# Chunked attention and a routed expert layer on one core: q and k of a tile in one transfer, V of two tiles in one

## The chip, the cores and the metric

The kernel runs on one core of a Trainium2 chip. The metric is the device time of one execution in microseconds (us). Engines are named as in the profile: PE is TensorE (matmul), PEld its weight load, DVE is VectorE, ACT is ScalarE, POOL is GpSimd, SP is SyncE, whose queue issues nearly all transfers between memory and SBUF. DMA share is the mean busy share of the core's 16 DMA engines.

## The reference

Inputs are q, k and v of 8 batches, 8 heads, 576 positions and 64 dimensions, in float32. Attention is computed in chunks of 64 positions. Its output, 4608 tokens of 512 values, goes through a layer of 8 experts: a token with a positive skip score is sent to its best expert, the others are passed through.

```python
scores = scale * np.matmul(q_c, k_c.transpose(0, 1, 2, 4, 3))   # chunks of 64
attn = np.exp(scores - max); attn = attn / (sum + 1e-09)
x = np.matmul(attn, v_c)                     # then 4608 tokens of 512
do_compute = x @ w_skip > 0
e_idx = np.argmax(x @ w_gate)                # of the tokens that compute
h = np.maximum(x @ w1[e], 0.0)
out = x + gate * (h @ w2[e])                 # of those; the others are x
```

## The kernel before, in words

The tokens are 36 tiles of 128 (NT, 128 rows each, two chunks of 64). The first stage, up to about 130 us, is the attention, in a loop over i from 0 to 38 that is a software pipeline: in iteration i, PE computes the scores of tile i (pe_scores, line 234, matmuls of line 241), transposes the probabilities of tile i-2 (pe_ptrans, line 273), multiplies those of tile i-3 with V (pe_pv, line 281, matmuls of line 289), transposes the output of tile i-4 (pe_xt, line 316), and computes router logits of older tiles (lines 328 and 341). ACT copies and exponentiates between these steps, DVE takes maxima and divides, POOL subtracts maxima. Routing work of groups of tiles is laid between. The second stage runs the experts' matmuls (lines 519 and 551), on tokens that POOL gathers from the output by indirect transfers, with weights loaded by SP in pieces of 512 KB (line 209).

The order of work on each engine is the order in which the program is written (a manual schedule), and a wait is put in by the framework where an instruction needs another's result or a buffer that is still in use. An engine that waits holds up everything behind it in its own order.

The input of a tile comes in three transfers, all issued by SP. load_q (line 124) takes a new buffer "st" out of five (QK_AHEAD) and loads q of the tile, 256 KB, 2048 bytes a partition; load_k (line 128) loads k into the other half of the same buffer; load_v (line 131) loads V with a column of ones, 260 KB, 2080 bytes a partition, into a buffer "sv" out of six (V_AHEAD). Ahead of the loop (lines 139 to 149) SP issues the first five q and k, the constants "csb" and "rsb", and six V. In the loop, q of tile i+5 is issued at the start of iteration i, behind pe_scores of tile i, which frees the buffer (line 735); the row of an output tile, or half a piece of expert weights, by side() (lines 304 to 310, and 360); V of tile i+3 behind pe_pv of tile i-3, which frees that buffer (line 766); and k of tile i+5 at the end (line 767).

SP's transfers take turns on eight semaphores (DMAHW0 to DMAHW7), and a transfer waits until the one eight before it on SP has landed. So at most eight of SP's transfers are in flight. PE starts with ten warm-up matmuls (line 160), with which the first loads run.

Of the kernel before, what the change touches and what calls it, by code (L numbers as in the profile page):

```python
# [9 lines left out]
F32 = mybir.dt.float32  # L10
# [8 lines left out]
P = 128  # L19
B, H, S, D = 8, 8, 576, 64  # L20
CH = 64
NTOK = B * S
NT = NTOK // P
# [3 lines left out]
KC = DM // P  # L27
# [28 lines left out]
QK_AHEAD = 5  # L56
V_AHEAD = 6
# [46 lines left out]
def moe_attention_kernel(ctx: ExitStack, tc: tile.TileContext, qk: bass.AP, vo: bass.AP, cst: bass.AP, crow: bass.AP, wall: bass.AP, out: bass.AP):  # L104
    nc = tc.nc
# [8 lines left out]
    ap = apool.__enter__()  # L114
# [5 lines left out]
    T = [dict() for _ in range(NT)]  # L120
    lgs = {}
    halves = (slice(0, CH), slice(CH, P))

    def load_q(t):
        T[t]["st"] = ap.tile([P, 2, DM], F32, name="st", bufs=QK_AHEAD)
        nc.sync.dma_start(T[t]["st"][:, 0], qk[0, t])

    def load_k(t):
        nc.sync.dma_start(T[t]["st"][:, 1], qk[1, t])

    def load_v(t):
        T[t]["sv"] = ap.tile([P, 2 * KC, D + 1], F32, name="sv", bufs=V_AHEAD)
        nc.sync.dma_start(T[t]["sv"].rearrange("p h d -> p (h d)"), vo[t])

    man = tc.manual_schedule()
    man.__enter__()
    csb = cpool.tile([P, CCOLS], F32, name="csb")
    rsb = cpool.tile([1, RCOLS], F32, name="rsb")
    for t in range(QK_AHEAD):
        load_q(t)  # L140
        load_k(t)
        if t == 1:
            nc.sync.dma_start(csb, cst)
        if t == 2:
            nc.sync.dma_start(rsb, crow)
        if t >= 2:
            load_v(t - 2)
    for t in range(QK_AHEAD - 2, V_AHEAD):
        load_v(t)
# [8 lines left out]
    def pe_warm(n):  # L158
        for _ in range(n):
            nc.tensor.matmul(warm, ones, zeros, start=True, stop=True)  # L160
# [32 lines left out]
    def more_constants():  # L193
        nc.vector.tensor_copy(upper, C("upper"))
        nc.vector.tensor_copy(cbase, C("cbase"))
        nc.vector.tensor_copy(recs[:, 0:2], C("tok").rearrange("p (c t) -> p c t", c=2))
        nc.vector.tensor_copy(dcon, csb[:, _C["wdesc"][0]:_C["iota"][1]])
        nc.vector.memset(ecum[:, 0, :], 0.0)
        nc.vector.memset(onesf, 1.0)
# [28 lines left out]
    def fill(q, budget):  # L228
        while q and budget >= 0.5 * q[0][0]:
            c, _, f = q.pop(0)  # L230
            f()
            budget -= c
# [59 lines left out]
    def ve_x(t):  # L292
        xq = T[t].pop("xq")[:, :, :XW].rearrange("p a (j d) -> p a j d", j=KC)
        rr = spool.tile([P, 2, KC, 1], F32, name="rr", bufs=2)
        nc.vector.tensor_scalar(rr, xq[:, :, :, D:], 1e-9, None, op0=ALU.add)
        nc.vector.reciprocal(rr, rr)
        x = ap.tile([P, DM], F32, name="xa", bufs=X_BUFS)
        nc.vector.tensor_tensor(x.rearrange("p (j a d) -> p a j d", a=2, d=D), xq[:, :, :, :D], rr.to_broadcast([P, 2, KC, D]), op=ALU.mult)  # L298
        rows.append((t, x))
        T[t]["x"] = x  # L300
# [3 lines left out]
    def side(i, n):  # L304
        for _ in range(n):
            if pieces and (pieces[0] < FC and i in W_AT or i >= BURST and pieces[0] >= FC and (not rows or pieces[0] <= (i - BURST) * 2 + FC)):
                load_half(pieces.pop(0))
            elif rows:
                t, x = rows.pop(0)
                nc.sync.dma_start(out[t * P:(t + 1) * P, :], x)  # L310
# [52 lines left out]
    def conv_half():  # L363
        st, hi, lo = cws.pop(0)
        nc.scalar.activation(hi, st, AF.Copy, scale=SW)
        fd.append((600, None, lambda: nc.vector.scalar_tensor_tensor(lo, st, SW, hi, op0=ALU.mult, op1=ALU.subtract)))

    def pool_lo():
        hi, st, lo = pl.pop(0)
        nc.gpsimd.tensor_tensor(lo, st, hi, op=ALU.subtract)  # L370
# [280 lines left out]
    def on(f, t):  # L651
        if 0 <= t < NT:
            f(t)
# [26 lines left out]
    def stage(g):  # L680
        next(jobs[g])
# [27 lines left out]
    def u0_mm():  # L709
        fc, n = u0[0], units[0][3]  # L710
        u0[0] += 1
        hp = u0_bank(fc)[:, :n]
        for m, (a, b, j) in enumerate((a, b, j) for a, b in ((0, 0), (0, 1), (1, 0)) for j in range(KC)):
            nc.tensor.matmul(hp, wsets[0][:, a, fc, j * P:(j + 1) * P], xt0[:, b, j, :n], start=(m == 0), stop=(m == 11))
        u0_ev.append((hp, fc))

    def u0_out():
        l1_out(ht0, *u0_ev.pop(0), units[0][3])

    def early_xt():  # L720
        return [blk_xt(xt0[:, :, :, m * P:(m + 1) * P], xgs[m], xp=u0_bank(m)) for m in range(2)]

    def do(i, spot):
        for f, a in spots.pop((i, spot), ()):
            f(*a)

    def conv_pool():
        st, hi, lo = cws.pop(0)
        nc.scalar.activation(st, st, AF.Copy, scale=SW)
        nc.scalar.activation(hi, st, AF.Copy)  # L730
        pl.append((hi, st, lo))

    for i in range(NT + 3):
        on(pe_scores, i)
        on(load_q, i + QK_AHEAD)
        if i == 2:
            more_constants()
        wm = WARM[i + 1] if i + 1 < len(WARM) else (0, 0, 0, 0)
        pe_warm(wm[0])
        on(ve_max, i - 1)  # L740
        if i != NT + 1:
            on(ve_x, i - 4)
        side(i, 1 if i < BURST else 2)
        if i % 2 == 0:
            on(ve_logit, i - 8)
        do(i, "d")
        if i == NT + 1:
            for f in lows:
                f()
        fill(fd, 600)  # L750
        do(i, "p")
        pe_warm(wm[1])
        on(ac_scores, i)
        on(pe_ptrans, i - 2)
        on(ac_pt, i - 2)
        do(i, "m")
        on(ac_exp, i - 1)
        pe_warm(wm[2])
        while pl:
            pool_lo()  # L760
        for c in range(W_CONV.count(i)):
            conv_half() if i < NT - 2 else conv_pool()
        pe_warm(wm[3])
        on(pe_pv, i - 3)
        if i >= 3:
            on(load_v, i - 3 + V_AHEAD)
        on(load_k, i + QK_AHEAD)
        if i >= BURST:
            side(i, 2)
        if i == NT + 2:  # L770
            ve_x(NT - 1)
            stage(5)
        if i % 2 == 0:
            on(pe_logit, i - 6)
            on(ac_logit, i - 6)
        if i % 2:
            on(pe_ltrans, i - 7)
        on(pe_xt, i - 4)
        on(ac_xt, i - 4)
        do(i, "e")  # L780
        if i == NT:
            ve_x(i - 3)
            scpool.__exit__(None, None, None)
            upool = tc.tile_pool(name="ps_u", bufs=1, space=PSUM, reuse_waits="tile")
            ps_u = upool.__enter__()
            lows = early_xt()
        if i > NT:
            u0_mm()
        if u0_ev and i > NT + 1:
            u0_out()  # L790
# [136 lines left out]
    for i, (p, bs, offs, n) in enumerate(units):  # L927
# [21 lines left out]
        for k, (b, o) in enumerate(zip(bs, offs)):  # L949
# [4 lines left out]
            for _ in l2_steps(y, hc, w, o, nb):  # L954
# [3 lines left out]
                if todo and at >= total - 1 - (TLEAD if i else LLEAD) * len(todo):  # L958
                    m, o2 = todo.pop(0)
# [45 lines left out]
def lay_out(q, k, v, moe_w_skip, moe_w_gate, moe_w1, moe_w2):  # L1005
    nch = S // CH

    def cols(a):
        a = a.reshape(B, KC, 2, nch, CH, D).transpose(0, 3, 5, 1, 2, 4).reshape(NT, 2, D, KC, 2, CH).copy()
        a[:, :, :, :, 1] = a[:, ::-1, :, :, 1]  # L1010
        return a.reshape(NT, P, DM)

    vv = v.reshape(B, KC, 2, nch, CH, D).transpose(0, 3, 2, 4, 1, 5).reshape(NT, 2, P, KC, D).transpose(0, 2, 1, 3, 4)
    vo = np.ones((NT, P, 2, KC, D + 1), np.float32)
    vo[..., :D] = vv
    vo = vo.reshape(NT, P, 2 * KC * (D + 1))
    qk = np.ascontiguousarray(np.stack([cols(q), cols(k)]))
    cst, crow = constants()
    wsg = np.concatenate([moe_w_skip[:, None], moe_w_gate], axis=1)
    lo, hi = _C["wsg"]  # L1020
    wp = np.zeros((P, KC, WP), np.float32)
    wp[:, :, :NE + 1] = wsg.reshape(KC, P, NE + 1).transpose(1, 0, 2)
    cst[:, lo:hi] = wp.reshape(P, -1)
    w1 = moe_w1.reshape(NE, KC, P, FC, P).transpose(0, 3, 2, 1, 4).reshape(NE, FC, P, KC * P)
    w2 = moe_w2.reshape(NE, FC, P, DM)
    wall = np.ascontiguousarray(np.concatenate([w1, w2], axis=3))
    return {"in_qk": qk, "in_vo": vo, "in_cst": cst, "in_crow": crow, "in_wall": wall}
# [14 lines left out]
```

## Time and profile before

| What | us |
|---|---|
| median of three runs | 350.34 (345.41 to 353.88) |
| profiled execution, its own time | 348.78 |
| its span, first to last instruction | 347.0 |
| PE busy in the span | 322.8 (93%) |
| DVE, ACT, POOL busy | 242.4, 195.1, 131.2 |
| q and k: 72 transfers of 256 KB, median from issue to landing | 5.0 |
| V: 36 transfers of 260 KB | 5.1 |
| output rows: 36 of 256 KB | 5.2 |
| weights: 56 of 512 KB | 4.2 |

The profile is of one execution. A row of the timeline gives the start, the length, the engine, the line and operation, the tiles written and read, and in square brackets how long the engine had been idle and what ended that; "issue" means that nothing in the profile explains it. A row of waits gives the engine and line, what it waited for, the total in us, how many times, and the longest. In the windows each engine has its busy time and in brackets its number of instructions; behind them stand the granted PE clock (1.00 is full speed), the DMA share and GB/s. In rows of transfers the last number is the median time from issue to landing in us. "q1 hardware_dynamic" is the queue of SP's transfers, "q8 instruction" one that carries program code.

### The profile page before, as it was taken

To read this page: it belongs to the slowest core of one execution; us is meant where nothing else is said; L and a number is where in the kernel's file an instruction comes from. 1 tells how busy PE (TensorE), PEld (TensorE's weight loads), DVE (VectorE), ACT (ScalarE), POOL (GpSimd) and SP (SyncE) were. 2 spreads that over 40 slices of the span, in tenths; PEclk is the share of its full clock that TensorE was granted. 3 is DMA by queue.
4 is the path that set the end of the run, shared out by engine and by line. 5 is a ranking of instruction groups with operands and counts; after the bars stand their busy time and mean duration, and the time that the engine had idled before them with its cause. 6 is when DMAs were issued, how large, how long until landed. Compare 5 with 4: busy or idle time off the path is not lost. (4 is left out here: it accounts for less than half of the span.)

```text
span 347.0 us, 10921 instructions
## 1 busy us (share of the span) xinstructions
PE 322.8 (93%) x4388; PEld 221.0 (64%) x4388; DVE 242.4 (70%) x539; ACT 195.1 (56%) x345; POOL 131.2 (38%) x158
## 2 busy tenths in 40 slices
PE   7889898998997999999999999999999999999980
PEld 3567676776675777659555446647647658587750
DVE  1645676987796887987889857876777779667420
ACT  3777787987784895516546344545444445455210
POOL 4423354463637456845050532242343353020111
PEclk9999999999998999999999999999999999999996
DMA  7999999998997992039375877668658767574000
GB/s 237 394 388 362 378 324 321 329 359 291 311 318 256 301 368 95 2 107 383 109 266 170 288 250 238 189 191 270 193 179 278 226 205 228 183 230 133 33 26 29
DMA packets 34408, 81.86 MB, mean 236 GB/s; under 512 B 4255, under 2 KB 4256, under 8 KB 34354
## 3 DMA queue, kind: packets, MB, share of 16 engines
q1 hardware_dynamic: 31250, 71.79, 62.1%
q0 software_dynamic: 3104, 9.33, 7.6%
q8 instruction: 36, 0.59, 0.7%
q14 instruction: 18, 0.15, 0.2%
HBM read 67.07 MB, written 14.17 MB: 234 GB/s over the span
## 5 line engine op out<-in xcount | busy, mean ns | idle before, releaser
L551 PE MATMUL sp<-wset,ht 128*128 128x512 f16 (+7 forms) x552 | 102.8, 379 | 0.0
L519 PE MATMUL hp<-xt,wset 128*128 128x288 f16 (+6 forms) x768 | 85.9, 273 | 0.9 <-DVE ht L528 0.9
L519 PEld LDWEIGHTS <-wset 128*128 128x128 f16 x768 | 69.3, 98 | 18.3 <-issue 3.4
L551 PEld LDWEIGHTS <-ht 128*128 128x128 f16 (+7 forms) x552 | 45.6, 101 | 45.1 <-issue 2.1
L218 DVE SCALAR_TENSOR_TENSOR wset<-wst,wset 128x1024 f16<-128x1024 f32 x56 | 67.6, 1217 | 9.2 <-ACT wset L217 9.1
L221 POOL DMA_INDIRECT out<-x,recsi x18 | 24.3, 1351 | 101.1 <-DVE x L561 87.7
L217 ACT ACTIVATE wset<-wst 128x1024 f16<-128x1024 f32 x56 | 57.8, 1048 | 1.8 <-DMA wst<-in_wall 1.8
L253 POOL TENSOR_TENSOR px<-sc,mx 128x512 f32<-128x512 f32 x36 | 38.0, 1058 | 53.4 <-DVE mx L251 30.6
L527 ACT ACTIVATE ht<-hp 128x288 f16<-128x288 f32 (+6 forms) x64 | 24.5, 383 | 56.0 <-PE hp L519 54.8
L528 DVE SCALAR_TENSOR_TENSOR ht<-hp,ht 128x288 f16<-128x288 f32 (+6 forms) x64 | 26.1, 422 | 17.9 <-ACT ht L527 17.3
L251 DVE TENSOR_REDUCE mx<-sc 128x8 f32<-128x512 f32 x36 | 24.4, 678 | 19.7 <-ACT sc L246 19.1
L503 ACT ACTIVATE xt<-xt 128x512 f16<-128x512 f32 (+7 forms) x20 | 10.3, 513 | 43.3 <-PE xt L502 43.3
L289 PE MATMUL xq<-sv,pz 64*64 64x65 f32 x1152 | 27.4, 226 | 6.5 <-issue 5.8
L289 PEld LDWEIGHTS xq<-sv,pz 64*64 64x64 f32 x1152 | 21.6, 135 | 13.6 <-issue 10.6
L241 PE MATMUL sc<-st 64*64 64x64 f32 x1152 | 25.9, 227 | 3.2 <-DMA st<-in_qk 1.8
L322 ACT ACTIVATE xc<-sp 128x512 f32<-128x512 f32 x36 | 21.4, 595 | 11.4 <-PE sp L316 10.1
L241 PEld LDWEIGHTS sc<-st 64*64 64x64 f32 x1152 | 20.9, 136 | 10.7 <-issue 4.6
L246 ACT ACTIVATE sc<-sc 128x512 f32<-128x512 f32 x36 | 21.5, 597 | 9.9 <-PE sc L241 8.6
L298 DVE TENSOR_TENSOR xa<-xq,rr 128x512 f32<-128x512 f32 x36 | 24.9, 692 | 1.2
L221 POOL DMA_INDIRECT xg<-out,recsi x18 | 23.2, 1287 | 5.5 <-issue 3.7
L273 PE MATMUL sp<-csb,px 128*128 128x128 f32 x144 | 23.9, 289 | 0.4 <-ACT sc L246 0.4
L506 DVE SCALAR_TENSOR_TENSOR xt<-xt 128x512 f16<-128x512 f32 (+7 forms) x20 | 11.7, 585 | 17.2 <-ACT xt L503 16.7
(157 smaller groups left out, 374.0 us busy)
## 6 DMA issues: line engine op xcount, KB each, us to landing
wst<-in_wall SPq DMA_DIRECT2D x56, 512.0 KB, 4.2
st<-in_qk SPq DMA_DIRECT2D x72, 256.0 KB, 5.0
sv<-in_vo SPq DMA_DIRECT2D x36, 260.0 KB, 5.1
out<-xa SPq DMA_DIRECT2D x36, 256.0 KB, 5.2
wst<-in_wall SPq DMA_DIRECT2D x16, 256.0 KB, 5.2
csb<-in_cst SPq DMA_DIRECT2D x1, 312.5 KB, 5.0
xg<-out,recsi POOLq DMA_INDIRECT x18, 5.6
out<-x,recsi POOLq DMA_INDIRECT x18, 4.8
```

What stands on the lines that cost most here:

```text
L217: nc.scalar.activation(w[:, 0, fc, :], st, AF.Copy, scale=SW)
L218: nc.vector.scalar_tensor_tensor(w[:, 1, fc, :], st, SW, w[:, 0, fc, :], op0=ALU.mult, op1=ALU.subtract)
L221: ins = nc.gpsimd.indirect_dma_start(**kw)
L241: nc.tensor.matmul(sp[halves[c], a, j], st[halves[r], 0, w], st[halves[r], 1, w], start=(j == 0), stop=True, skip_group_check=True)
L251: nc.vector.tensor_reduce(mx, T[t]["sc"], axis=AX.X, op=ALU.max)
L253: nc.gpsimd.tensor_tensor(px, T[t].pop("sc"), mx.unsqueeze(2).to_broadcast([P, H, CH]), op=ALU.subtract)
L289: nc.tensor.matmul(xq[w, a, j * (D + 1):(j + 1) * (D + 1)], pz[r, j, w], v[r, c, j], start=(j == 0), stop=True, skip_group_check=True)
L298: nc.vector.tensor_tensor(x.rearrange("p (j a d) -> p a j d", a=2, d=D), xq[:, :, :, :D], rr.to_broadcast([P, 2, KC, D]), op=ALU.mult)
L519: nc.tensor.matmul(hp, w()[:, a, fc, j * P:(j + 1) * P], xt[:, b, j, :n], start=(m == 0), stop=(m == 11))
L527: nc.scalar.activation(ht[:, 0, fc, :n], hp, AF.Relu)
L528: nc.vector.scalar_tensor_tensor(ht[:, 1, fc, :n], hp, 0.0, ht[:, 0, fc, :n], op0=ALU.max, op1=ALU.subtract)
L551: nc.tensor.matmul(y[c * P // cg:c * P // cg + n], ht[:, a, fc, o:o + n], w[:, b, fc, P * KC:], start=(f == 0 and m == 0), stop=(f == fw - ...
```

## The change

q and k of a tile lie side by side in memory and are loaded by one transfer of 512 KB, 4096 bytes a partition, into the same buffer "st" as before. V of two tiles lies side by side and is loaded by one transfer of 520 KB, 4160 bytes a partition (532 thousand bytes), into one of three buffers of double size. Nothing else is changed; the arrays are laid out for it on the host before the launch.

```diff
-    def load_q(t):
+    def load_qk(t):
         T[t]["st"] = ap.tile([P, 2, DM], F32, name="st", bufs=QK_AHEAD)
-        nc.sync.dma_start(T[t]["st"][:, 0], qk[0, t])
-
-    def load_k(t):
-        nc.sync.dma_start(T[t]["st"][:, 1], qk[1, t])
+        nc.sync.dma_start(T[t]["st"].rearrange("p a m -> p (a m)"), qk[t])
 
     def load_v(t):
-        T[t]["sv"] = ap.tile([P, 2 * KC, D + 1], F32, name="sv", bufs=V_AHEAD)
-        nc.sync.dma_start(T[t]["sv"].rearrange("p h d -> p (h d)"), vo[t])
+        if t % 2 == 0:
+            vp = ap.tile([P, 2, 2 * KC, D + 1], F32, name="sv", bufs=V_AHEAD // 2)
+            T[t]["sv"], T[t + 1]["sv"] = vp[:, 0], vp[:, 1]
+            nc.sync.dma_start(vp.rearrange("p t h d -> p (t h d)"), vo[t // 2])
...
     for t in range(QK_AHEAD):
-        load_q(t)
-        load_k(t)
+        load_qk(t)
...
         on(pe_scores, i)
-        on(load_q, i + QK_AHEAD)
+        on(load_qk, i + QK_AHEAD)
...
         on(pe_pv, i - 3)
-        if i >= 3:
-            on(load_v, i - 3 + V_AHEAD)
-        on(load_k, i + QK_AHEAD)
+        if i >= 4 and i % 2 == 0:
+            on(load_v, i - 4 + V_AHEAD)
```

SP at the start of the program, before the change. A row is an instruction of SP with its line, the tile (with its buffer's number) that it writes, what it reads, and in brackets the semaphores that it waits for; DMAHW ones are those of earlier transfers, PE and DVE those of the engines that use a buffer:

```order
L126 DMA st_86<-in_qk 128x512
L129 DMA st_86<-in_qk 128x512
L126 DMA st_89<-in_qk 128x512
L129 DMA st_89<-in_qk 128x512
L143 DMA csb_84<-in_cst 128x625
L126 DMA st_93<-in_qk 128x512
L129 DMA st_93<-in_qk 128x512
L145 DMA rsb_85<-in_crow 1x366
L133 DMA sv_97<-in_vo 128x520 [waits DMAHW0_49]
L126 DMA st_99<-in_qk 128x512 [waits DMAHW1_49]
L129 DMA st_99<-in_qk 128x512 [waits DMAHW2_49]
L133 DMA sv_102<-in_vo 128x520 [waits DMAHW3_49]
```

and with the change:

```order
L126 DMA st_86<-in_qk 128x1024
L126 DMA st_88<-in_qk 128x1024
L141 DMA csb_84<-in_cst 128x625
L126 DMA st_91<-in_qk 128x1024
L143 DMA rsb_85<-in_crow 1x366
L132 DMA sv_94<-in_vo 128x1040
L126 DMA st_96<-in_qk 128x1024
L126 DMA st_98<-in_qk 128x1024
L132 DMA sv_100<-in_vo 128x1040 [waits DMAHW0_49]
L132 DMA sv_102<-in_vo 128x1040 [waits DMAHW1_49]
L126 DMA st_161<-in_qk 128x1024 [waits DMAHW2_49,PE_49]
```

The first eight transfers, which wait for nothing, were q and k of three tiles and the constants, and are now those of five tiles, the constants and the first pair of V.

SP in the loop before the change, from q of one iteration to that of two iterations later:

```order
L126 DMA st_391<-in_qk 128x512 [waits DMAHW7_49,PE_49]
L310 DMA out_0<-xa_400 128x512 [waits DMAHW0_49,DVE_49]
L133 DMA sv_430<-in_vo 128x520 [waits DMAHW1_49,PE_49]
L129 DMA st_391<-in_qk 128x512 [waits DMAHW2_49]
L126 DMA st_456<-in_qk 128x512 [waits DMAHW3_49,PE_49]
L310 DMA out_0<-xa_465 128x512 [waits DMAHW4_49,DVE_49]
L133 DMA sv_495<-in_vo 128x520 [waits DMAHW5_49,PE_49]
L129 DMA st_456<-in_qk 128x512 [waits DMAHW6_49]
L126 DMA st_529<-in_qk 128x512 [waits DMAHW7_49,PE_49]
```

and with the change, the same places:

```order
L126 DMA st_435<-in_qk 128x1024 [waits DMAHW3_49,PE_49]
L308 DMA out_0<-xa_444 128x512 [waits DMAHW4_49,DVE_49]
L132 DMA sv_474<-in_vo 128x1040 [waits DMAHW5_49,PE_49]
L126 DMA st_507<-in_qk 128x1024 [waits DMAHW6_49,PE_49]
L308 DMA out_0<-xa_516 128x512 [waits DMAHW7_49,DVE_49]
L126 DMA st_571<-in_qk 128x1024 [waits DMAHW0_49,PE_49]
```

Two iterations had eight transfers and now have five: k stands where q was, ahead of the output row and V, and V comes in every second iteration.

More of the change, by code (lines that the diff above doesn't have):

```diff
@@ L1015, in lay_out @@
     vo[..., :D] = vv
-    vo = vo.reshape(NT, P, 2 * KC * (D + 1))
-    qk = np.ascontiguousarray(np.stack([cols(q), cols(k)]))
+    vo = vo.reshape(NT // 2, 2, P, 2 * KC * (D + 1)).transpose(0, 2, 1, 3).reshape(NT // 2, P, 4 * KC * (D + 1)).copy()
+    qk = np.concatenate([cols(q), cols(k)], axis=2)
     cst, crow = constants()
```

## The prediction

> **What bounds the kernel now.** I read the busy time in windows first, then the waits of TensorE (PE), then the timeline around the longest of them, then the transfers. The windows of the first 150 us, where q, k and V are loaded (columns: PE, PEld, DVE, ACT, POOL, then the granted clock, the DMA engines' busy share, GB/s):
>
> ```profile
> 0.00:10.00 10.00, 7.84 (x114) 3.81 (x115) 2.19 (x10) 3.47 (x6) 4.07 (x11) 1.00 0.79 259
> 10.00:20.00 10.00, 7.81 (x218) 5.62 (x216) 4.78 (x11) 6.49 (x12) 4.13 (x4) 1.00 1.05 388
> 100.00:110.00 10.00, 7.89 (x195) 5.98 (x188) 7.38 (x24) 6.12 (x12) 5.57 (x6) 0.90 0.91 307
> 140.00:150.00 10.00, 10.00 (x69) 5.95 (x67) 9.42 (x33) 3.91 (x8) 7.53 (x11) 1.00 0.01 2
> ```
>
> The DMA engines are full from 10 us on, and PE has gaps. From 140 us PE has none and the DMA engines idle, so what the change does must be done before then. One tile's q, k, V and output are 1028 KB, at 388 GB/s 2.71 us of transfer. PE needs more: two tiles lie between these starts of scores, 5.82 us, so 2.91 us a tile.
>
> ```profile
> 33.73 0.69 PE L241 MATMUL sc<-st 64*64 64x64 f32 x32
> 39.55 0.64 PE L241 MATMUL sc<-st 64*64 64x64 f32 x28
> ```
>
> So PE sets the pace, with transfers 7% behind it. PE's own long waits, from the list of waits and the timeline:
>
> ```profile
> PE xq L289 <- issue: 5.8, 4, 2.0
> PE sc L241 <- DMA st<-in_qk: 1.8, 2, 1.6
> PE sc L241 <- issue: 0.6, 1, 0.6
> 18.28 0.41 PE L241 MATMUL sc<-st 64*64 64x64 f32 x13 [1.58 <-DMA st<-in_qk]
> 31.45 0.33 PE L241 MATMUL sc<-st 64*64 64x64 f32 x2 [0.58 <-issue]
> 42.48 0.34 PE L289 MATMUL xq<-sv,pz 64*64 64x65 f32 x7 [1.21 <-issue]
> 53.52 0.33 PE L289 MATMUL xq<-sv,pz 64*64 64x65 f32 x4 [1.35 <-issue]
> 79.35 0.44 PE L289 MATMUL xq<-sv,pz 64*64 64x65 f32 x10 [1.26 <-issue]
> 107.16 0.51 PE L289 MATMUL xq<-sv,pz 64*64 64x65 f32 x18 [1.99 <-issue]
> ```
>
> Data is late once, at tile 5 (18.28 us). The other five, 0.58 and 5.81 us, are "issue": PE stops inside a run of like matmuls and no semaphore explains it. Counting the matmuls between these stops does (column PE):
>
> ```profile
> 14.50:31.40 16.90, 14.27 (x377) 1.00 1.04 386
> 31.40:42.45 11.05, 9.70 (x251) 1.00 1.04 365
> 42.45:53.50 11.05, 9.58 (x253) 1.00 0.95 335
> 53.50:79.30 25.80, 24.33 (x630) 1.00 0.98 335
> 89.80:107.10 17.30, 15.21 (x378) 1.00 0.96 328
> ...
> q8 instruction: 36, 0.59, 0.7%
> ```
>
> They are 3, 2, 2, 5 and 3 times 126, and a matmul has its weight load: PE stops at boundaries of blocks of about 256 instructions. The last row, of the page, is a queue of 36 instruction transfers, 0.59 MB, 16 KB each. So PE's code comes in blocks by the same DMA engines, and a block that is late stops PE. How late it is follows the data queue. After a stop PE has run dry, and the next block can be asked for no earlier than its restart. After the restart at 31.45 us I looked for the packet of 16 KB, and at the landing of data issued then; and the same after 79.35 us (V of 31.13 us, 31.45 to 34.05, 34.05 to 35; V of about 79 us, 79.35 to 80.55, 80.55 to 82):
>
> ```profile
> sv<-in_vo SPq DMA_DIRECT2D x1, 260.0 KB, 5.2
> DMA packets 520, 0.95 MB, mean 365 GB/s; under 512 B 59, under 2 KB 59, under 8 KB 520
> q8 instruction: 1, 0.02, 6.1%
> ...
> sv<-in_vo SPq DMA_DIRECT2D x1, 260.0 KB, 3.8
> DMA packets 207, 0.37 MB, mean 309 GB/s; under 512 B 26, under 2 KB 26, under 8 KB 207
> q8 instruction: 1, 0.02, 5.3%
> ```
>
> In the first stretch all 520 packets are under 8 KB, and the block's packet follows after 2.6 us; data took 5.2 us. In the second it follows after 1.2 us; data took 3.8 us. Both differ by 2.6 us: the block seems to stand in line behind the data already issued, and that is the step on which I put most weight.
>
> **The Trainium skill** (DMA: Bandwidth & Descriptors, Queues, rings and completion order) says that each DMA engine goes round robin between its queue rows, packet by packet, so that a code block would pass long data queues. By that rule the startup stall below would not come and the time would be that of rival A. The two rows above, 2.6 and 1.2 us, speak against it, without excluding it. The skill (Runtime: NRT & Kernel Launch, Instruction fetch mechanics) also describes 16 KB blocks of 256 instructions, fits the counts above, and calls the cost mostly hidden; here 5.8 us are not.
>
> **The change part by part.** *Longer rows, 4096 and 4160 bytes for 2048 and 2080.* The nearest row for long packets is a stretch in which weights of 4096 bytes a partition arrive, with some gathers:
>
> ```profile
> 156.00:161.00 5.00, 5.00 (x58) 5.00 (x57) 3.71 (x6) 3.20 (x7) 2.44 (x2) 1.00 1.03 419
> ```
>
> Per unit of busy share that is 419/1.03 = 407 GB/s, against 388/1.05 = 370 at 10 to 20 us: up to 9% less DMA time on the 772 KB of q, k and V, so 0 to 0.19 us a tile; as other packets are mixed in, I take half, 0.1 us. PE sets the pace, so this pays only at tile 5, where six tiles are 0.6 us (0 to 1.1) earlier, of 1.58 us.
>
> *Fewer issues.* 36 of 72 q/k issues and 18 of 36 V issues go, at the 0.33 us of the rows below some 18 us of SP's queue. SP is off the path, since from 45 to 98 us it waits mostly for buffers that PE frees:
>
> ```profile
> SPq L126 <- PE sc L241: 8.1, 12, 1.1
> ```
>
> Worth 0. If that cover went, 0.33 us an issue would count, as a gain.
>
> *A tile's k is issued with its q, V in pairs.* k moves ahead of the output row, the V load and the weight half of its iteration; those land later by at most one 256 KB transfer, 0.66 us. V of a pair waits for the later of two freed buffers, and is used 5 iterations after its issue rather than 6, some 14 us against a landing of about 5 us. Worth 0. Nothing is behind these waits on SP that was not behind them before.
>
> *More bytes in flight at the start.* SP lets eight transfers be in flight. Now the first eight are 1850 KB, with the change 3394 KB (five q/k tiles, the constants, a V pair). The early issues, and the first code block:
>
> ```profile
> 4.46 0.50 SPq L133 DMA_DIRECT2D sv<-in_vo  x1
> 6.17 0.33 SPq L129 DMA_DIRECT2D st<-in_qk  x1
> 6.83 0.33 SPq L133 DMA_DIRECT2D sv<-in_vo  x1
> ...
> DMA packets 981, 1.80 MB, mean 390 GB/s; under 512 B 108, under 2 KB 109, under 8 KB 981
> q8 instruction: 1, 0.02, 5.9%
> ...
> 14.64 0.41 PE L273 MATMUL sp<-csb,px 128*128 128x128 f32 x2 [0.39 <-ACT sc L246]
> ```
>
> That block's packet lies in the stretch from 12.0 to 13.1 us (none of the 981 packets between 7.4 and 12 is one), and three blocks of 126 before the stop at 31.4 us its boundary is at 14.5 us, where PE goes on at 14.64. Two of the late blocks have their packets in these stretches, 40.0 to 41.2 and 104.8 to 105.8 us:
>
> ```profile
> q8 instruction: 1, 0.02, 5.4%
> ...
> q8 instruction: 1, 0.02, 5.7%
> ```
>
> Their stops end at 42.48 and 107.16 us, about 1.4 us after; 13.1 + 1.4 = 14.5 us: the first block is just in time. I estimate that it was asked for one block before, around 7.4 us. By then eight q/k halves, the constants and two V loads were issued, 2.95 MB; at 259 GB/s up to 10 us and 388 over the last 2.6, 1.58 MB had been moved. So 1.4 MB stood ahead, 3.5 us. With the change the eight free slots and the next two V pairs let 4434 KB, 4.54 MB, be issued by then: 2.96 MB ahead, 7.6 us. The block comes 4.0 us later, at 18.5 us, and PE stands still for 3.9 us (0 if blocks pass the data; 5.5 if q5 and k5 are in line as well).
>
> Part of it is paid back. Tile 5's data has landed by then. PE had 2.1 us of work between 14.6 us and the data wait, so tile 5 starts at 18.5 + 2.1 = 20.6 instead of 18.28 us: +2.3 us. PE is then later by that much while the transfers go on, 0.9 MB less in line, and the blocks that were late at 31.45 us and 42.48 us are in time: -0.6 and -1.2. Between ends of 0 and -2.3 I take -1.8. Net of the start: +0.5 us.
>
> *The clock.* The 1.99 us stop at 107 us was followed by this stretch (PE busy 3.40 us, clock column 0.52):
>
> ```profile
> 107.90:111.30 3.40, 3.40 (x54) 2.62 (x56) 2.60 (x10) 1.40 (x3) 1.40 (x7) 0.52 0.79 238
> ```
>
> Half a clock for 3.4 us costs 1.7 us. A stop of 3.9 us is twice as long, so I count 1.7 us for it; 0 if the stop is shorter, 3.4 if there are two.
>
> *Blocks after 50 us.* Both kernels are paced by freed buffers there. Longer rows shorten the line, pairs make it lumpier. I take 0, between -4.6 us (no late block at 53.5, 79.4 and 107 us) and +5 us (14 blocks later by 0.35 us, half a V transfer).
>
> Sum: -0 for rows (their 0.6 us lies inside the stop) + 0.5 + 1.7 + 0 = +2.2 us on a profiled time of 348.78 us (its span is 347.0, and 1.8 us lie around it): 351.0. That execution is 1.6 us under the median of the three runs, 350.34, which spread over 8.5 us. As its own stop at 107 us and its clock may or may not recur, I write 350.5 us: no change that a measurement of this kernel, about 2%, can tell.
>
> **The rivals.** *A: the blocks pass the data, or the startup line is shorter than I count.* Then only the longer rows act: 0.6 to 1.6 us at tile 5, 348.78 - 1.1 = 347.7 us. For it: 14.64 us is put down to ScalarE, not to code. Against: the four landing and packet times. *B, slower: every block is late.* The place is PE's boundary every 126 matmuls, some 18 of them from 31 to 131 us. If one lump (q/k 512 KB, output 256 KB, V 520 KB in one iteration, 1288 KB against 1028) stands ahead of a block at each request, it is 260 KB, 0.66 us, later each time: 18 x 0.66 = 11.9 us, less 1.1: 359.6 us. It decides from a line of more than about 1.1 MB (the 2.6 us above) at the request. For it: blocks have no slack now, since four are late and others just in time. Against: in half of the iterations the lump is smaller than now, 768 KB. *C, faster: the transfers get ahead.* With 5 to 9% less DMA time the line is short whenever PE asks, the waits of 5.8 and 1.58 us and the 1.7 us of the clock go: 348.78 - 9.1 = 339.7 us. For it: transfers are only 7% faster than PE now. Against: lines are set by buffers, not by speed, and the start is worse. *D: the rows stay short in the hardware*, so that nothing but the order changes: the forecast without its first term. Weights of 4096 bytes a row already arrive faster (419 GB/s), so I give it no chance of its own.
>
> **How the numbers follow.** Forecast 0.52, A 0.24, B 0.14, C 0.10. Faster by over 2%, under 343.3 us, are half of C: 0.05. Slower by over 2%, above 357.3, are most of B, and a little of the forecast's own range: 0.11. The rest, 0.84, is within 2%. The range takes in A (347.7) and the spread of runs below it, and B up to half of its price: 345.0 to 357.0; outside lie C and the upper half of B, with a little of the runs' own spread.
>
> **What would show it.** Right: PE's first stop by "issue" near 14 us grows to 3 to 5 us, the wait for tile 5's data is gone, half a clock for 3.4 us follows, landing times at the start are near 8 us instead of 5, and the loading stage's DMA engines reach 400 GB/s. The start of the block's packet, 12 us now, tells most: near 16 us by the forecast, near 12 by A. Wrong: PE passes 14.6 us without a stop, or the sum of "issue" waits after 50 us moves by more than 5 us either way.

## The result, and the profile after

| | before | after |
|---|---|---|
| median of 20 executions each, us | 348.69 (344.42 to 353.88) | 351.70 (348.82 to 356.54) |
| profiled execution: its own time, us | 348.78 | 350.85 |
| its span, us | 347.0 | 349.0 |

The ratio of after to before is 1.0124, 95% interval 1.0088 to 1.0161: slower by 1.2%, some 4 us, and no difference by the bound of 2%. Executions more than 1.5% above the fastest of their kernel are left out of every ratio here, so a ratio differs from that of the medians, which take in all executions, by up to 0.7%.

The lines of after are two less than before's (scores 239, the matmul with V 287). The windows of after, in the columns of before's windows, and last the row of before from 20 to 30 us:

```profile
0.00:10.00 10.00, 7.93 (x113) 3.87 (x114) 3.18 (x10) 3.46 (x6) 4.10 (x11) 1.00 0.84 312
10.00:20.00 10.00, 8.99 (x234) 6.43 (x234) 5.96 (x14) 7.90 (x14) 5.18 (x5) 1.00 1.02 406
20.00:30.00 10.00, 8.33 (x219) 5.98 (x218) 4.63 (x13) 6.71 (x12) 2.49 (x4) 1.00 1.01 373
100.00:110.00 10.00, 9.20 (x241) 7.15 (x238) 7.29 (x27) 7.44 (x16) 4.03 (x4) 1.00 0.95 299
...
20.00:30.00 10.00, 9.62 (x252) 7.04 (x242) 6.41 (x17) 8.29 (x16) 3.90 (x4) 1.00 1.04 384
```

From 10 to 20 us the transfers are faster, 406 GB/s at a share of 1.02 against 388 at 1.05, and PE does 234 matmuls where it did 218. It is better off up to 20 us and no more behind that: from 20 to 30 us PE does 219 where it did 252. Packets, q/k and V, from the page of after, and its granted clock in 40 slices of 8.7 us:

```profile
PEclk9999999999999999999999999999999999999997
DMA packets 26631, 81.85 MB, mean 235 GB/s; under 512 B 3391, under 2 KB 3392, under 8 KB 26578
st<-in_qk SPq DMA_DIRECT2D x36, 512.0 KB, 5.0
sv<-in_vo SPq DMA_DIRECT2D x18, 520.0 KB, 6.3
out<-xa SPq DMA_DIRECT2D x36, 256.0 KB, 6.2
```

The long rows are real: 26631 packets for 34408. The clock is full until the very end. The waits of PE by "issue" in after, and from its timeline the start and every stop by "issue" behind it:

```profile
PE sc L239 <- issue: 3.7, 4, 1.3
PE xq L287 <- issue: 3.0, 4, 1.2
PE rk L410 <- issue: 0.9, 1, 0.9
PE sp L314 <- issue: 0.9, 1, 0.9
PE sp L271 <- issue: 0.8, 1, 0.8
PE sp L326 <- issue: 0.6, 1, 0.6
```

```profile
14.53 0.66 PE L271 MATMUL sp<-csb,px 128*128 128x128 f32 x4 [0.50 <-ACT sc L244]
...
16.77 0.69 PE L239 MATMUL sc<-st 64*64 64x64 f32 x32
...
20.93 0.56 PE L239 MATMUL sc<-st 64*64 64x64 f32 x20 [1.29 <-issue]
26.27 0.39 PE L287 MATMUL xq<-sv,pz 64*64 64x65 f32 x9 [0.51 <-issue]
32.37 0.21 PE L239 MATMUL sc<-st 64*64 64x64 f32 x1 [1.10 <-issue]
43.35 0.46 PE L287 MATMUL xq<-sv,pz 64*64 64x65 f32 x13 [1.22 <-issue]
59.25 0.49 PE L271 MATMUL sp<-csb,px 128*128 128x128 f32 x3 [0.76 <-issue]
70.04 0.56 PE L287 MATMUL xq<-sv,pz 64*64 64x65 f32 x19 [1.05 <-issue]
75.52 0.39 PE L239 MATMUL sc<-st 64*64 64x64 f32 x10 [0.62 <-issue]
86.43 0.24 PE L410 MATMUL rk<-eh,ones 128*128 128x36 f16 x4 [0.90 <-issue]
92.58 0.27 PE L314 MATMUL sp<-csb,xa 128*128 128x128 f32 x1 [0.88 <-issue]
97.68 0.58 PE L287 MATMUL xq<-sv,pz 64*64 64x65 f32 x24 [0.20 <-issue]
103.17 0.46 PE L239 MATMUL sc<-st 64*64 64x64 f32 x15 [0.68 <-issue]
119.28 0.62 PE L326 MATMUL sp<-xc,csb 128*32 128x256 f32 x3 [0.56 <-issue]
```

Three things are to be seen. The wait for tile 5's data is gone: its scores start at 16.77 us, not 18.28. What was gained is gone one block of code later: PE meets the next boundary early, its code is not there, and the stop of 1.29 us ends at 20.93 us, where the same matmul started at the same time before. And from there PE stops for code twelve times, each time at a multiple of 126 matmuls (within two), where before it stopped six times (the five of the prediction and 0.43 us at 89.85). The sum of these rows is 9.8 us against 6.8.

**Where the difference lies.** The first 2912 matmuls of PE are the same, in the same order, in all kernels of this study; the last of them starts at about 136 us in the kernel before. For each kernel I summed, from the records of PE's instructions, what the matmuls at the 22 boundaries of code blocks up to there start later than at the usual pace, and half of the time in which the clock was granted at one half. The last column is the mean time from PE's restart behind such a gap (of over 0.25 us, before 130 us) to the start of the next block's packet:

| Kernel (one profiled execution each) | 2912th matmul at, us | stops at boundaries | half of half clock | what is left | restart to next block, us (restarts) |
|---|---|---|---|---|---|
| before | 136.0 | 8.7 | 1.7 | 125.6 | 2.32 (9) |
| after | 137.3 | 12.4 | 0 | 124.9 | 2.71 (14) |
| q and k merged, V as before (e1) | 137.8 | 14.2 | 0 | 123.6 | 2.38 (11) |
| V pairs only (e2) | 141.6 | 11.9 | 3.4 | 126.3 | 2.65 (11) |
| q and k merged, short rows (e3) | 137.2 | 11.5 | 1.7 | 124.0 | 2.83 (13) |
| transfers of 64 partitions (e4) | 165.2 | 23.5 | 15.4 | 126.3 | 4.11 (11) |
| two V issued together (e5) | 139.4 | 10.3 | 5.1 | 124.0 | 2.33 (11) |
| k right behind q (e6) | 132.0 | 6.9 | 0 | 125.1 | 2.37 (9) |
| e1 with four buffers (e7) | 133.9 | 6.2 | 3.4 | 124.3 | 2.17 (7) |
| q, k loaded for five tiles only (e8) | 126.1 | 3.5 | 0 | 122.6 | 2.16 (2) |
| V pairs by two transfers (e9) | 136.7 | 9.5 | 1.7 | 125.5 | 2.41 (12) |
| after, slots as before (e10) | 137.6 | 11.4 | 1.7 | 124.5 | 2.57 (11) |
| after, four buffers (e11) | 141.4 | 12.2 | 5.1 | 124.1 | 2.80 (10) |
| k right behind q, four buffers (e12) | 134.3 | 6.6 | 1.7 | 126.0 | 2.11 (7) |

The 2912th matmul moves by 39 us between kernels, and what is left by 3.7. From there to the end of the span it is 210.2 to 211.7 us in all but e8, whose later stages do other work. So most of what a kernel gains or loses here lies in the loading stage, at the boundaries of code and in the clock. For the change itself, whose loss of some 4 us is no larger than what is left varies, the table tells less: in these two executions PE is 1.3 us later at the 2912th matmul and the span is 2.0 us longer. One execution of a kernel is not its median (e1's profiled execution was 1.5 us above it, e6's 2.3 us below), so the size of an effect is taken from the ratios, and only its kind from this table. The stops alone don't go with the ratios told below: e1 has 14.2 us of them and is as fast as the kernel before, with 8.7. The last column does: 2.57 to 2.83 us in the five kernels that are slower by 1.0 to 1.6%, 2.41 in e9 (0.8%), 2.11 to 2.38 in the kernel before and the five that are as fast as it, within 0.5%. But the single waits lie between 1.1 and 4.4 us (e4 apart), so such a mean is uncertain by some 0.2 to 0.4 us, about as much as these means differ.

### The profile page after: what moved, and what is told of

Read it like the earlier page. It is cut to its first block, busy times and chain, and to the rows that moved or that the text cites. A ratio compares the mean times of both kernels' runs of the same rounds, so it can differ in the third digit from the quotient of the medians.

```text
span 349.0 us, 10836 instructions
## 1 busy us (share of the span) xinstructions
PE 322.1 (92%) x4388; PEld 219.9 (63%) x4388; DVE 242.5 (69%) x539; ACT 194.7 (56%) x345; POOL 130.7 (37%) x158
## 2 busy tenths in 40 slices
DMA packets 26631, 81.85 MB, mean 235 GB/s; under 512 B 3391, under 2 KB 3392, under 8 KB 26578
## 5 line engine op out<-in xcount | busy, mean ns | idle before, releaser
L501 ACT ACTIVATE xt<-xt 128x512 f16<-128x512 f32 (+7 forms) x20 | 10.3, 513 | 43.8 <-PE xt L500 43.8
L287 PE MATMUL xq<-sv,pz 64*64 64x65 f32 x1152 | 26.6, 224 | 3.6 <-issue 3.0
L239 PEld LDWEIGHTS sc<-st 64*64 64x64 f32 x1152 | 20.8, 135 | 11.9 <-issue 7.9
L276 ACT ACTIVATE pz<-sp 128x512 f32<-128x512 f32 x36 | 21.5, 597 | 5.1 <-PE sp L271 4.2
```

What stands on the lines that cost most here:

```text
L239: nc.tensor.matmul(sp[halves[c], a, j], st[halves[r], 0, w], st[halves[r], 1, w], start=(j == 0), stop=True, skip_group_check=True)
L287: nc.tensor.matmul(xq[w, a, j * (D + 1):(j + 1) * (D + 1)], pz[r, j, w], v[r, c, j], start=(j == 0), stop=True, skip_group_check=True)
```

## The experiments

All kernels of one group ran beside the kernel before on one chip, groups e1 to e4, e5 to e8 and e9 to e12. The theory on record was that a block of code waits behind the bytes in line, so that larger lumps, issued at once, make it later.

### Each half of the change alone, and the rows apart from the merging

e1: q and k as in the change, V as before. Of the diff of the change only this stays:

```diff
+        nc.sync.dma_start(T[t]["st"].rearrange("p a m -> p (a m)"), qk[t])
```

> Only q and k of a tile in one 512 KB transfer; V as before. Theory 'line' (a code block stands behind the bytes that are in line when it is asked for, and larger transfers make the line lumpier): about half of the change's loss, ratio to before 1.005 to 1.010, PE's waits by issue some 8 us against 6.8 before and 9.9 with the whole change. Theory 'packets' (a block waits for a certain number of packets, so longer packets make it later): two thirds of the long packets are here, ratio 1.008. Theory 'startup' (the prediction's: the first block is late because more is in flight at the start): the first eight transfers are 3134 KB, so nearly the whole loss, ratio 1.012, and the loss is there before 30 us.

Measured: 348.29 against 348.01 us, ratio 1.003 (0.9983 to 1.0078).

e2: V in pairs as in the change, q and k as before:

```diff
+            nc.sync.dma_start(vp.rearrange("p t h d -> p (t h d)"), vo[t // 2])
```

> Only V in pairs of 520 KB; q and k as before. Line: the other half of the loss, ratio 1.003 to 1.008, since a pair puts 520 KB in line at once in every second iteration. Packets: a third of the loss, ratio 1.004. Startup: the first eight transfers are as large as before, ratio 1.000, no loss before 30 us.

Measured: 353.66 against 348.01 us, ratio 1.0159 (1.0075 to 1.0242). V's pairs carry the loss, and for q and k merged no cost is seen.

e3: q and k of a tile by one transfer, but from two separate arrays, so that a row stays 2048 bytes:

```diff
+        nc.sync.dma_start(T[t]["st"], qk[:, t].rearrange("a p m -> p a m"))
```

> q and k of a tile in one transfer of 512 KB, but in rows of 2048 bytes as before (the arrays as before, one transfer over both); V as before. Line: as q and k alone in long rows, ratio 1.005 to 1.010, or a little more as the short rows take longer to move. Packets: the packets are those of before, ratio 1.000 (within 0.4%). Startup: as q and k alone.

Measured: 350.68 against 348.01 us, ratio 1.0135 (1.0061 to 1.0208). Against e1, where only the rows are longer, that is 1.05% more; with the two half widths, 0.74 and 0.48, added in squares it is 0.2 to 1.9%, 0.6 to 6.7 us. So longer rows are worth some 3.6 us, and the merging with short rows costs some 4.7. By the medians, 348.29 and 350.68, both are smaller, 2.4 and 2.7 us.

e4: 4096-byte rows in transfers of 256 KB as before, one for each half of the partitions:

```diff
+        nc.sync.dma_start(T[t]["st"][:CH].rearrange("p a m -> p (a m)"), qk[t, :CH])
...
+        nc.sync.dma_start(T[t]["st"][CH:].rearrange("p a m -> p (a m)"), qk[t, CH:])
```

> Rows of 4096 bytes as in the change, but a tile's q and k in two transfers of 256 KB, each of 64 partitions, at the places where q and k were issued before; V as before. Line: transfers, places and bytes in line are those of before and move a little faster, ratio 0.995 to 1.000. Packets: as q and k alone in one transfer, ratio 1.008. Startup: the first eight transfers are as large as before, ratio 0.995 to 1.000.

Measured: 377.81 against 348.01 us, ratio 1.0926 (1.0846 to 1.1007). No theory on record has that. Its windows (the columns as before), the same windows of the kernel before, and e4's transfers:

```profile
10.00:50.00 40.00, 29.49 (x640) 21.34 (x641) 15.69 (x41) 19.81 (x36) 10.04 (x10) 0.87 1.05 271
50.00:90.00 40.00, 33.63 (x765) 25.30 (x764) 24.14 (x73) 25.45 (x49) 13.10 (x20) 0.87 1.05 256
...
10.00:50.00 40.00, 35.40 (x925) 26.14 (x924) 23.70 (x67) 29.81 (x55) 14.65 (x19) 1.00 1.03 374
50.00:90.00 40.00, 36.49 (x951) 27.64 (x950) 32.25 (x93) 32.83 (x62) 19.17 (x32) 1.00 0.94 321
```

```profile
st<-in_qk SPq DMA_DIRECT2D x72, 256.0 KB, 7.4
sv<-in_vo SPq DMA_DIRECT2D x36, 260.0 KB, 7.1
```

The DMA engines are full, 1.05, and move 271 and 256 GB/s, where they moved 374 and 321. A packet of 4096 bytes takes 286 ns (median, 10 to 50 us), in e1 159 ns. So this form of transfer is slow by itself, and the run tells nothing about row length. With the slower data code comes later: PE's stops are 23.5 us, the most of all.

Of the three theories, "packets" falls with e3 (1.000 expected) and "startup" with e1 (1.012) and e2 (1.000). "Line" comes nearest, though e2 lies above its range of 1.003 to 1.008 and e1 a little under 1.005.

### Lumps in the order of issue

e5: V as before, one transfer a tile into a buffer of its own, but two of them issued together in every second iteration, where the change issues a pair:

```diff
-        if i >= 3:
-            on(load_v, i - 3 + V_AHEAD)
+        if i >= 4 and i % 2 == 0:
+            on(load_v, i - 4 + V_AHEAD)
+            on(load_v, i - 3 + V_AHEAD)
```

> V stays in single transfers of 260 KB with 2080 bytes a partition, but two are issued one behind the other in every second iteration, where the pair would be; the first loads are as before. If V in pairs costs because 520 KB come into line at once in every second iteration (theory 'line'): ratio to before 1.010 to 1.020, like V in pairs alone (1.016), and PE's waits by issue 9 to 10 us against 6.8. If it costs because of the one large transfer itself (a pair lands as a whole, longer rows), ratio 1.000.

Measured: 348.69 against 347.92 us, ratio 0.9975 (0.9927 to 1.0023). The lump of 520 KB in the order of issue costs nothing.

e6: k issued right behind its q, as the change has it, as two transfers:

```diff
         on(load_q, i + QK_AHEAD)
+        on(load_k, i + QK_AHEAD)
...
-        on(load_k, i + QK_AHEAD)
```

> k of a tile is issued right behind its q, as 256 KB of its own, ahead of the output row and V; all else as before. Line: the lump of 512 KB is that of the merged transfer, so the ratio is that of q and k in one transfer with short rows, 1.006 to 1.013. If the merged transfer costs for what it is, or for the larger first eight transfers: ratio 1.000.

Measured: 346.41 against 347.92 us, ratio 0.9954 (0.9914 to 0.9995). It is rather a gain. So the theory of lumps falls: issuing the same bytes together does no harm. And e3 differs from e6 in one thing: two transfers of 256 KB, one behind the other, are one of 512 KB (on one of SP's eight slots for two), with the same rows in the same place. PE then has fewer semaphore instructions, 114 for 130, so that e3's code boundaries come to lie up to 8 matmuls later; they lie where those of e1 do (within one), which is not slower. The ratios are 1.0135 and 0.9954, each against the kernel before in its own group, their intervals are apart, and the difference, 1.8%, is some 6 us (1.2%, some 4 us, by the medians). For q and k, then, one larger transfer costs what two smaller ones don't.

### Fewer bytes ahead, and no bytes

e7: e1 with four buffers for q/k and four for V, for five and six:

```diff
-QK_AHEAD = 5
-V_AHEAD = 6
+QK_AHEAD = 4
+V_AHEAD = 4
```

> q and k in one transfer as in the change, V single, and four tiles ahead of both (it was five of q and k and six of V): 1.04 MB less to load at the start. Startup part of the theory (a long line when the first blocks are asked for): the stops near 14 and 21 us, 3.0 and 1.8 us with q and k merged alone, shrink by 1 to 2 us, ratio to before 0.995 to 1.000. If lines are set by lumps only: ratio as with five and six, 1.000 to 1.003.

Measured: 348.33 against 347.92 us, ratio 1.0004 (0.9967 to 1.0042). The stops at the first two boundaries are gone, a wait of 1.5 us for data has come, and the time is the same, as the second expectation had it.

e8: the kernel before, but q and k are loaded for the first five tiles only; later tiles use those again. This leaves out 62 of 72 loads of q and k, and all that follows from their values is different, so its total of 523 us isn't compared. PE does the same matmuls up to about 130 us:

```diff
+        if t >= QK_AHEAD:
+            T[t]["st"] = kept[t % QK_AHEAD]
+            return
```

> The kernel before, but q and k are loaded for the first five tiles only and used again for all others, so half of the loads' bytes are left out in the attention stage; its scores, and so the routing and the time of the experts, are not those of the reference, and only the first 130 us are compared. If late code blocks are due to data in line: PE's waits by issue after 20 us fall from 6.1 us to under 1.5 us, and the experts' matmuls begin some 6 to 8 us earlier. If blocks are late for another reason (the code fetch itself is too slow for PE here): the waits stay, 5 us or more.

Measured, the windows of e8 and all of PE's waits from 20 to 135 us:

```profile
10.00:50.00 40.00, 36.31 (x992) 27.05 (x990) 25.23 (x69) 31.52 (x58) 16.44 (x23) 1.00 0.65 208
50.00:90.00 40.00, 39.52 (x1057) 30.18 (x1047) 35.35 (x102) 36.15 (x69) 21.20 (x32) 1.00 0.60 178
```

```profile
PE sp L335 <- ACT pz L285: 0.4, 1, 0.4
PE sp L335 <- ACT xc L329: 0.3, 1, 0.3
PE xq L296 <- PE sp L280: 0.2, 1, 0.2
```

No stop by "issue" is left behind 20 us, PE is busy 39.52 of 40 us from 50 us on, and the 2912th matmul is at 126.1 us for 136.0, though the first block stopped PE for 3.0 us. Data itself was not what PE waited for behind 20 us in the kernel before, so this shows the mechanism: a block of code comes late because data is on the DMA engines, and in the kernel before that costs, with the half clock behind one of the stops, about 10 us of 348 in this pair of executions.

### What is it about the pair: buffers, slots or size

e9: V's pair buffer and its place as in e2, but filled by two transfers of 260 KB:

```diff
+            nc.sync.dma_start(vp[:, 0].rearrange("p h d -> p (h d)"), vo[t])
+            nc.sync.dma_start(vp[:, 1].rearrange("p h d -> p (h d)"), vo[t + 1])
```

> q and k as before; V of two tiles into one buffer of double size as in the change, so that both are freed and waited for together, but by two transfers of 260 KB with 2080-byte rows, issued one behind the other. S (the size of one transfer costs): no loss, 0.995 to 1.004 of the time before, as with the two V transfers issued together into separate buffers (0.9975). L (a pair that lands and comes free together costs): 1.01 to 1.02, as with one transfer for the pair (1.0159). F (the eight slots hold more bytes when transfers are larger): no loss, since the slots hold what they held before; S and F are told apart by the next run.

Measured: 350.29 against 347.39 us, ratio 1.0076 (1.0040 to 1.0112), between the two expectations. Against e5 (0.9975), which in the loop issues the same transfers at the same place into separate buffers, the pair buffer, whose two tiles come free together and are waited for together, costs about 1.0% (0.6% by the medians). The rest up to e2's 1.0159 would be the single transfer; e2's and e9's intervals overlap, so for V that rest isn't shown. How the pair buffer costs its part isn't either: PE never waits for V's data in e9, and SP's wait for V's buffer is no longer than before. From SP's waits between 10 and 131 us, of before and of e9:

```profile
SPq L133 <- PE xq L289: 11.8, 9, 4.1
```

```profile
SPq L135 <- PE xq L292: 11.3, 10, 6.4
```

e10: the changed kernel, with a transfer of 512 bytes that nobody reads behind each q/k and each V pair, so that two iterations take eight of SP's slots, as before:

```diff
+        nc.sync.dma_start(ap.tile([1, 128], F32, name="nul", bufs=8), crow[:, :128])
```

> The changed kernel with a transfer of 512 bytes, whose data nobody reads, behind each q/k and each V pair, so that two iterations take eight of SP's slots as before, and the first eight transfers hold three tiles' q and k, not five. F (bytes in flight): the loss goes, 0.995 to 1.004 of the time before, and the line at 12 us is near 1.5 MB instead of 2.3 to 3.0. S (size of one transfer) and L (joint landing of V): the loss stays, 1.009 to 1.016, since the transfers and buffers are those of the change. 36 + 18 more issues on SP are off the path by both.

Measured: 352.07 against 347.39 us, ratio 1.0105 (1.0052 to 1.0159). What was issued and not yet moved at 12 us is 1.1 MB, in after 2.2, and the loss stays. So the bytes in flight that the slots allow aren't the cause.

e11: the changed kernel with four buffers for q/k and two V pairs.

> The changed kernel with four buffers for q and k instead of five and two V pairs instead of three (QK_AHEAD 4, V_AHEAD 4), so 772 KB fewer can be issued ahead. F' (what matters is how many bytes the buffers let stand in line): faster than the change, 0.995 to 1.005 of the time before, with fewer stops after 20 us. S: the loss stays, 1.009 to 1.016. L: larger loss, 1.015 to 1.03, since a V pair that is freed late is then used three iterations after its issue instead of five, and waits for data appear at the matmuls with V.

Measured: 351.91 against 347.39 us, ratio 1.0101 (1.0048 to 1.0154). The loss stays again, so it isn't the depth of the buffers either. The larger loss expected under L, 1.015 to 1.03, did not come.

e12: e6 with four buffers and four.

> The kernel before with k issued right behind its q (0.9954 alone) and four buffers for q and k and for V instead of five and six. If the line that the buffers allow makes the blocks of code late: 0.98 to 0.993, with the stops at the first two block boundaries gone and fewer behind them. If the line in the loop is set by what each iteration moves and not by the buffers ahead: 0.994 to 1.000, the stops after 20 us as with k issued early alone, some 5 to 7 us. If four buffers are too few, waits for data come at scores and at the matmuls with V: over 1.005.

Measured: 348.12 against 347.39 us, ratio 1.0032 (0.9995 to 1.0069). Less ahead gains nothing in the form of e6 either. The fastest version stays e6, 346.41 us, by 0.5% in one comparison.

## Why the prediction came near, and which step failed

Forecast 350.5 us, measured 351.70, within 2% as held likely. The number is near by luck: terms were wrong in opposite ways. By the prediction's own sign of being wrong, PE passing 14.6 us without a stop, its account of the start failed: PE is idle there for 0.50 us, behind ScalarE, and was for 0.39. Point by point:

**PE sets the pace, and late blocks of code are its loss: right.** e8 shows it.

**Longer rows, -0.6 us at tile 5: the place right, the size too small.** The 1.58 us at tile 5 went, and 406/1.02 = 398 GB/s a unit of share is 7.6% over the 370 of before, inside 0 to 9%. But "this pays only at tile 5" was too little: from e3 to e1 the rows are worth some 3.6 us (2.4 by the medians). How is not shown: less late blocks in the loop would be one way, but e1's profiled execution has more stops than e3's, 14.2 us for 11.5, though shorter waits behind a restart, 2.38 for 2.83.

**Fewer issues, and a tile's k issued with its q, 0: right.** SP waits for scores between 10 and 131 us 49.7 us in after and 9.7 us before, so the time that it saved is stood through, and e6 puts k's early issue at 0 to -3 us.

```profile
SPq L126 <- PE sc L239: 49.7, 27, 3.2
```

```profile
SPq L126 <- PE sc L241: 9.7, 14, 1.1
```

**V in pairs, 0: failed.** The argument was that V is used late enough and that nothing new stands behind the wait for its buffer. By e9's rows both hold (SP's longest wait there is 6.4 us, for 4.1), and it costs 2.6 us (1.4 to 3.9) all the same (e9), 5.5 us (2.6 to 8.4) with the single transfer (e2).

**The first block behind the line, +0.5 us, and the clock, +1.7 us: failed, and it is the step on which most weight was put: "the block seems to stand in line behind the data already issued".** The line was what I had counted: at 7.4 us 3.0 to 3.1 MB were issued and not moved (2.96 by the prediction), before 1.4. The block came at the same time, at 12.04 us for 12.01 before. In after, the transfers from 4 to 12 us, and those of the next 0.1 us; then the same 0.1 us of the kernel before:

```profile
DMA packets 958, 3.31 MB, mean 413 GB/s; under 512 B 104, under 2 KB 105, under 8 KB 958
...
q1 hardware_dynamic: 958, 3.31, 102.9%
```

```profile
DMA packets 14, 0.05 MB, mean 538 GB/s; under 512 B 4, under 2 KB 4, under 8 KB 13
...
q8 instruction: 1, 0.02, 62.1%
```

```profile
DMA packets 24, 0.05 MB, mean 534 GB/s; under 512 B 5, under 2 KB 5, under 8 KB 23
...
q8 instruction: 1, 0.02, 65.4%
```

At 413 GB/s the 4.6 us from 7.4 to 12.04 us move 1.9 MB, so if the block was asked for when I estimated, it passed about 1.1 MB of data issued before it. With no long stop at 14.5 us no half clock followed. The Trainium skill (DMA: Bandwidth & Descriptors, Queues, rings and completion order) has a DMA engine go round robin between its queue rows, packet by packet; that the block passed data agrees with it, and rival A rested on it. Yet A's time, 347.7 us, was missed as well, since PE's stops in the loop grew instead of staying as they were. And the line isn't without weight there: over the nine restarts of the kernel before the wait is about 1.4 us and 1.2 us for each MB in line (correlation 0.80), where a line served in order would be 2.6 us a MB at 388 GB/s. Over some 140 such restarts of all fourteen kernels it is about 0.9 us and 1.9 us for each MB (correlation about 0.65), and by kernel, without e4 and e8, from 1.1 (e6) to 3.1 us (e9) for each MB. So for the loop these runs don't tell how much of the data ahead of it a block passes.

**What is paid back, -1.8 us: failed too.** The blocks that were late at 31.45 and 42.48 us were to come in time. They stop PE for 1.10 and 1.22 us, for 0.58 and 1.21 before, and stops of 1.29 and 0.51 us at 20.93 and 26.27 us are new. Of the 3.7 us that the stops grow, 2.4 lie ahead of 50 us. At 42 to 48 us PE is 0.9 us later, near the +0.5 of the prediction by other terms: 1.5 us gained at tile 5, and 2.4 lost at blocks behind it.

**Blocks after 50 us, 0 between -4.6 and +5: the sign was left open, and the size was small here.** The stops are shorter and twice as many, 1.2 us more in sum. As the 1.7 us of half clock in the kernel before don't recur, PE is 1.3 us later at the 2912th matmul, 0.5 us more than at 48 us. Rival B had this direction and the wrong reason: it was to come from lumps of bytes in the order of issue, and e5 and e6 each issue one of these lumps at no cost (no run has both).

**What stays open.** Shown are that data on the DMA engines makes code late (e8), that one transfer of 512 KB costs more than two of 256 KB (e3 against e6; one profile of each has 11.5 and 6.9 us of stops), that a pair buffer for V, filled by two transfers, costs about 1% (e9 against e5), and that neither slots (e10) nor buffers ahead (e11, e12) carry the loss. Why a larger transfer costs, and whether it does so by delaying blocks of code, is not shown. One reading is that a DMA engine serves its share of one transfer to the end before it turns to the code's queue; the restarts would fit it, 2.83 us to the next packet in e3 and 2.37 in e6. But a mean over 7 to 14 restarts is not sharp, the bytes in line at them differ a little too (1.07 MB in e3, 0.85 in e6), and the records don't tell which DMA engine carried a packet; so it stays a guess.

## What to carry to other kernels

Where PE runs a long unrolled program beside full DMA engines, look for its stops by "issue" and count the matmuls between them: here equal counts meant code that came late, and the form of the transfers mattered though no engine waited for data. Merging loads paid by longer rows and cost by larger transfers and by buffers that come free in pairs; try each alone, since here q and k broke even and V lost. A gain ahead of a late block of code can be lost at that block, as tile 5's 1.5 us were.

## What was not expected of the hardware

- **The first block of code comes at different times, by no cause that these runs show.** Its packet comes between 11.9 and 12.6 us in eight of the fourteen profiled executions, at 13.6 us in e1, and between 14.4 and 15.4 us in e5, e8, e10 and e12 (at 17.9 us in e4, where all is slow). e5 issues the same transfers as the kernel before up to 13 us, and at 14 us e8 has 0.6 MB in line. In e5 the block lies in the 0.2 us from 15.0 us, and PE's row behind it is

```profile
q8 instruction: 1, 0.02, 32.5%
```

```profile
17.74 1.08 PE L273 MATMUL sp<-csb,px 128*128 128x128 f32 x4 [3.07 <-issue]
```

  A stop of 3 us, not far from the 3.9 us that the prediction had for the change, thus came with the same data issued as in the kernel before; whether it comes and goes between executions of one kernel, whose times spread over 7.7 us (after) and 9.5 us (before), is not shown.
- **Transfers of 64 partitions with 4096-byte rows are slow:** in e4, with V and the output mixed in, 271 and 256 GB/s at a full share, against 374 and 321 in the same windows of the kernel before.
- **Packets of long rows are 5 to 6% cheaper a byte:** in the records a packet of 2048 bytes takes 84 ns (median) and one of 4096 bytes 159 ns.
